# Softmax steps, M's combinations and w_out's block sums issued at other places in a fused recurrent-cross attention and SERF MLP kernel

## The chip, the cores and the metric

The kernel runs on one core of a Trainium2 chip. The metric is the device time of one execution in microseconds (us). One execution of the kernel before is laid open by the hardware profiler; all times inside the kernel that this document names come from that trace, counted from the start of its span.

Five engines matter: PE (TensorE, the matmuls; PEld is its weight load), DVE (VectorE), ACT (ScalarE), POOL (GpSimd) and SP (SyncE, which issues the DMAs). Each engine works through its own list of instructions in order; engines wait for each other through semaphores.

## The reference, cut to what matters

```python
def _attn_ref(x, state):                       # x (8, 8, 512, 64), state (8, 8, 32, 64)
    scale = 1.0 / np.sqrt(D)
    scores = scale * np.matmul(x, state.transpose(0, 1, 3, 2))
    a = softmax(scores)                        # (written out in the original)
    xread = np.matmul(a, state)
    scores2 = scale * np.matmul(state, x.transpose(0, 1, 3, 2))
    a2 = softmax(scores2)
    sread = np.matmul(a2, x)
    return np.concatenate([xread, sread], axis=2)

def _moe_ref(x, w_in, w_out):                  # x (4352, 512), w_in (512, 2048), w_out (2048, 512)
    h = x @ w_in
    sp = np.maximum(h, 0.0) + np.log1p(np.exp(-np.abs(h)))
    g = h * erf(sp)
    return g @ w_out
# the attention output, heads side by side, is the x of the second part; all in float32
```

## The kernel before

The eight batches are taken one after the other. For the 512 rows that come from `xread`, the kernel never forms the attention output: it multiplies M = state x w_in (made per batch, `mixed`) with the attention weights `aT`. Both large products, M x aT (the hidden layer h) and g x w_out, are done block-wise with seven products in place of eight (a fast 2 x 2 scheme), which needs sums of blocks: `combine_m` (of M), `combine_a` (of aT) and `combine_w` (of w_out, once for the whole kernel).

From batch 1 on a batch has four **groups**, g = 0 to 3. A group makes 512 hidden features for 256 tokens (`hidden7`, seven products of 128-column matmuls), applies softplus, Erf and the product with h (`finish`), and is multiplied into the output (`project7`, seven products of 256-column matmuls). The project step of a group is run one group later: its pieces are laid between the products of the next group's `hidden7`.

```python
    def hidden7(b, g, h, between):
        hs = act.tile([P, 4, S], F32, name="hs")
        s = act.tile([P, 4, S], F32, name="s")
        c11, c12, c21, c22 = (hs[:, k] for k in range(4))
        m1, u2, u3 = s[:, 3], c12, c21
        ...                                     # product(n, bank): matmuls, L457; softplus(k): L464
        add = lambda o, x, y: nc.vector.tensor_tensor(o, x, y, op=ALU.add)      # L465
        p, q = (ps_h.tile([P, S], F32, name="h") for _ in range(2))             # two PSUM banks
        product(1, p)
        nc.scalar.copy(m1, p)                   # L468
        product(6, q)
        add(u2, m1, q)
        between()
        product(2, p, False)                    # adds onto bank p: only after m1 was copied
        nc.scalar.copy(c11, p)                  # L473
        product(7, q, False)                    # adds onto bank q: only after u2
        add(u3, m1, q)
        softplus(0)
        between()
        p, q = (ps_h.tile([P, S], F32, name="h") for _ in range(2))             # the same two banks
        product(5, p)                           # only after c11 was copied
        add(c22, u3, p)
        product(4, q)                           # only after u3
        add(c21, u3, q)
        between()
        marks[:] = product(3, p, False), add(c12, u2, p)    # the group's last add; only after c22
        for k in (3, 2, 1):
            softplus(k)
        return s, hs

    def finish(s, hs):
        return (nc.scalar.activation(out=s, in_=s, func=ACTF.Erf),              # L507
                nc.vector.tensor_tensor(s, s, hs, op=ALU.mult))                 # L508

    def combine_w(g, last=False):               # block sums of w_out, L539; T[4], T[3] as the others
        ...
        if last:
            sub(T[3], B22, B12)
        else:
            sub(T[1], B12, B11)
            sub(T[2], B22, T[1])
            sub(T[4], B21, T[2])

    def project7(gT, hs, g, first, last, acc):  # L561 to L564 form S1..S4 on DVE, L565 the matmuls
        ...
        for n, (lhs, rhs, bank, c) in enumerate((
                (A12, B21, 0, 0), (A11, B11, 2, 0), (A22, T[4], 1, 0), (S2, T[2], 0, 1),
                (S3, T[3], 2, 1), (S1, T[1], 1, 1), (S4, B22, 3, 0))):
            ...
```

The softmaxes of batch b + 1 (`attention`) run inside the groups of batch b, in steps: scores (PE L197, copied by ACT L207), the maxima and first exponentials (DVE L217 to L221, ACT L222), the second exponentials (DVE L238 and L239, ACT L246), normalising and turning (DVE L228 to L233, L353), turning of the second weights (DVE L356 and DMAs) and the state read (PE L273, DVE L279). `combine_m` is DVE L397 to L400, `combine_a` L428 to L431, `mixed` PE L385 with copies on ACT L387 and DVE L388, and `store7` ACT L576 and DVE L575.

Where a step is issued is decided by the main loop. `side[n]` runs a step behind piece n of the pending project; pieces 0 to 2 lie inside `hidden7`, later ones behind it. `behind(marks, f)` makes the instructions of f be ordered behind the instructions in `marks`.

```python
    for b in range(1, B + 1):
        ...
        for g, (first, second) in enumerate(groups):
            side = {}
            if b < B and g == 0:
                side[2] = lambda turn=turn: next(turn)          # state read of this batch
            if b + 1 < B:
                if g == 0:
                    turn = attention(b + 1)
                    side[6 if b > 1 else 3] = lambda: behind(marks, next, turn)   # scores
                elif g == 1:
                    side[0] = lambda: [next(turn) for _ in range(4)]   # all other softmax steps
                else:
                    o = g - 2 ^ begins(b + 1)
                    side[4] = lambda: mixed(b + 1, 2 * o)
                    side[8] = lambda: (mixed(b + 1, 2 * o + 1), combine_m(b + 1, o))
                    if g == 3:
                        side[6] = lambda: combine_a(b + 1)
            ...                                                  # the last batches: not touched
            steps = accompanied(pending(), side)
            gT_ = first(lambda: next(steps))
            if b == 1 and g == 0:
                combine_m(1, 1 - begins(1))
                behind(marks, combine_w, begins(1))
            done(steps)
            if b == 1 and g == 0:
                combine_w(begins(1), True)
            if b == 1 and g == 1:
                behind(marks, combine_w, 1 - begins(1))
                behind(marks, combine_w, 1 - begins(1), True)
            ...
```

Up to batch 0's end (the first 122 us) the kernel loads and converts the weights and takes another, plain path; after batch 7 come the 256 rows of the states. Neither is touched.

Of the kernel before, what the change touches and what calls it, by code (L numbers as in the profile page):

```python
# [16 lines left out]
def kernel(  # L17
# [17 lines left out]
    nc = tc.nc  # L35
    B, H, S, D = x.shape
# [151 lines left out]
    marks = []  # L188
# [183 lines left out]
    def mixed(b, g, *copies):  # L372

        m_t[b, g] = mix.tile([P, 2, gw], F32, name="m")
        mixed_part(b, g, 0, 1, *copies)
# [14 lines left out]
    def combine_m(b, g):  # L390


        (X11, X12), (X21, X22) = ([m_t[b, 2 * g + j][:, e] for e in range(2)] for j in range(2))
        sx = mix.tile([P, 3, gw], F32, name="sx", bufs=2)
        S1, S2, S4 = (sx[:, k] for k in range(3))
        tt = nc.vector.tensor_tensor
        tt(S1, X21, X22, op=ALU.add)  # L397
        tt(S2, S1, X11, op=ALU.subtract)
        tt(X21, X11, X21, op=ALU.subtract)
        tt(S4, X12, S2, op=ALU.subtract)  # L400
        X[b, g] = X11, X12, S4, X22, S1, S2, X21
# [32 lines left out]

    X, Ys = {}, {}

    def hidden7(b, g, h, between):

# [6 lines that stand above are left out]
        def product(n, bank, first=True):  # L447
            x, y = X[b, g][n - 1], Ys[b][n - 1]
            for i in range(GF):
                q = slice(P * i, P * i + P)  # L450
                if b < B:
                    ops = [(x[:, q], y[:, h])]
                else:
                    ops = [(x[:, i // 2, k, P * (i % 2):P * (i % 2) + P], y[:, k])
                           for k in range(2)]
                for k, (lhsT, rhs) in enumerate(ops):
                    last = nc.tensor.matmul(out=bank[:, q], lhsT=lhsT, rhs=rhs,  # L457
                                            start=(first and i == 0 and k == 0),
                                            stop=(i == GF - 1 and k == len(ops) - 1),
                                            skip_group_check=not first)  # L460
            return last

        def softplus(k):
            nc.scalar.activation(out=s[:, k], in_=hs[:, k], func=ACTF.Softplus)  # L464
        add = lambda o, x, y: nc.vector.tensor_tensor(o, x, y, op=ALU.add)  # L465
        p, q = (ps_h.tile([P, S], F32, name="h") for _ in range(2))
        product(1, p)
        nc.scalar.copy(m1, p)  # L468
        product(6, q)
        add(u2, m1, q)  # L470
        between()
        product(2, p, False)
        nc.scalar.copy(c11, p)  # L473
        product(7, q, False)
        add(u3, m1, q)
        softplus(0)
        between()
        p, q = (ps_h.tile([P, S], F32, name="h") for _ in range(2))
        product(5, p)
        add(c22, u3, p)  # L480
        product(4, q)
        add(c21, u3, q)
        between()
        marks[:] = product(3, p, False), add(c12, u2, p)
# [3 lines that stand above are left out]
# [41 lines left out]
    B11, B12, B21, B22 = (wb[:, :, h, :, c, :] for h in range(2) for c in range(2))  # L529
    T = {}  # L530

    def combine_w(g, last=False):

        if not T:
            for k in 1, 2, 4:
                T[k] = act.tile([P, 2 * GF * P * 2], U32, name="raw", bufs=3).bitcast(F32) \
                    .rearrange("p (g i e) -> p g i e", i=GF, e=E2)
            T[3] = B12
        sub = lambda o, x, y: nc.vector.tensor_tensor(o[:, g], x[:, g], y[:, g], op=ALU.subtract)  # L539
        if last:  # L540
            sub(T[3], B22, B12)
        else:
            sub(T[1], B12, B11)
            sub(T[2], B22, T[1])
            sub(T[4], B21, T[2])

    def project7(gT, hs, g, first, last, acc):


        blocks = lambda t: [t[:, k].rearrange("p (i t) -> p i t", i=GF) for k in range(4)]  # L550
        A11, A21, A12, A22 = blocks(gT)
        S1, S2, S3, S4 = blocks(hs)
        tt = nc.vector.tensor_tensor
        for n, (lhs, rhs, bank, c) in enumerate((
                (A12, B21, 0, 0), (A11, B11, 2, 0), (A22, T[4], 1, 0), (S2, T[2], 0, 1),
                (S3, T[3], 2, 1), (S1, T[1], 1, 1), (S4, B22, 3, 0))):
            for i in range(GF):
                if i % 2 == 0 and n:
                    yield
                if i == 2 and n == 1:  # L560
                    tt(S1, A21, A22, op=ALU.add)  # L561
                    tt(S2, S1, A11, op=ALU.subtract)  # L562
                    tt(S3, A11, A21, op=ALU.subtract)
                    tt(S4, A12, S2, op=ALU.subtract)  # L564
                nc.tensor.matmul(out=acc[bank][:, E2 * c:E2 * c + E2], lhsT=lhs[:, i, :],  # L565
                                 rhs=rhs[:, g, i, :], start=(first and i == 0 and c == 0),
                                 stop=(last and i == GF - 1 and (c == 1 or bank == 3)))
# [37 lines left out]
    def begins(b):  # L605
        return 1 - b % 2

    def fast(b, parts, put):
        for h in range(parts):
            box = []  # L610

            def project_(gT, k, g, h, box):
                if k == 0:
                    box.extend(tiles(4))
                yield from project7(*gT, g, k == 0, k == 1, box)
                if k == 1:
                    store7(box, put(h))

            def first(g, h, between):
                gT = hidden7(b, g, h, between)  # L620
                finish(*gT)
                return gT
            for k in range(2):
                g = k ^ h ^ begins(b)
                yield lambda between, g=g, h=h: first(g, h, between), \
                    lambda gT, k=k, g=g, h=h, box=box: project_(gT, k, g, h, box)

    def done(steps):
# [9 lines left out]
    def behind(marks, f, *args):  # L638
        with ExitStack() as order:
            for m in marks:  # L640
                order.enter_context(tc.issue_after(m.ins))
            return f(*args)
# [97 lines left out]
    acc = tiles(NC)  # L740
# [85 lines left out]
    xT, _ = turn_x(1)  # L826
# [6 lines left out]
    turn = attention(1, xT)  # L833
# [51 lines left out]
    for b in range(1, B + 1):  # L885
        if b < B:
            groups = fast(b, 2, lambda h, b=b: put_x(b, h))
        else:
            groups = fast(b, 1, lambda h: put_s)
        for g, (first, second) in enumerate(groups):  # L890
            side = {}
            if b < B and g == 0:
                side[2] = lambda turn=turn: next(turn)
            if b + 1 < B:

                if g == 0:
                    turn = attention(b + 1)
                    side[6 if b > 1 else 3] = lambda: behind(marks, next, turn)
                elif g == 1:
                    side[0] = lambda: [next(turn) for _ in range(4)]  # L900
                else:
                    o = g - 2 ^ begins(b + 1)
                    side[4] = lambda: mixed(b + 1, 2 * o)
                    side[8] = lambda: (mixed(b + 1, 2 * o + 1), combine_m(b + 1, o))
                    if g == 3:
                        side[6] = lambda: combine_a(b + 1)
            elif b + 1 == B and g == 1:
                side[4] = lambda: [turn_read(range(k, min(k + 4, B))) for k in range(0, B, 4)]
            elif b + 1 == B and g > 1:

                if g == 2:
                    side[6] = lambda: combine_a(B)
                side[8] = lambda: combine_s(g - 2 ^ begins(B))
            steps = accompanied(pending(), side)
            gT_ = first(lambda: next(steps))
            if b == 1 and g == 0:
                combine_m(1, 1 - begins(1))
                behind(marks, combine_w, begins(1))
            done(steps)
            if b == 1 and g == 0:  # L920
                combine_w(begins(1), True)
            if b == 1 and g == 1:
                behind(marks, combine_w, 1 - begins(1))
                behind(marks, combine_w, 1 - begins(1), True)

            def pending(gT=gT_, second=second):
                return second(gT)
# [31 lines left out]
```

## Time and profile before

| what | value |
|---|---|
| time, median of 3 runs | 751.2 us (749.37 to 752.59) |
| span of the profiled execution | 749.4 us |
| granted TensorE clock, mean | 0.998 |
| PE busy | 730.8 us, 98% of the span |
| PE weight load busy | 584.4 us, 78% |
| DVE busy | 522.2 us, 70% |
| ACT busy | 388.6 us, 52% |

A busy share tells how long an engine had an instruction in it. Matmuls overlap in PE's pipeline, so a busy PE need not be a PE at its best rate; how fast it really goes is read from the timeline, as the distance from the start of one run of matmuls to the start of the next. Where PE stood and waited is told in the view of waits and in the timeline, in square brackets behind a run of matmuls, with the engine and line that released it.

In the trace a product of four matmuls of the program appears as eight, so a product of `hidden7` is "L457 ... x8", and one of `project7` "L565 ... x8".

### The profile page before, as it was taken

Reading aid. Unit: us, or ns where it says so; the run is one execution under the profiler, and the core shown is the slowest. Engines: PE = TensorE matmul, PEld = TensorE weight load, DVE = VectorE, ACT = ScalarE, POOL = GpSimd, SP = SyncE. Lnnn points to the kernel's source line nnn. Section 1 sums busy time; section 2 is a strip of 40 time slices with the busy share of each in tenths; the row PEclk is TensorE's granted clock in tenths of the full one; section 3 lists DMA queues with packets and bytes.
Section 4 is the critical chain, followed back from the end, with each engine's and each line's share of the span. In section 5 each row is a group of like instructions: output and inputs, shape, how many; then the busy total and the mean of one; then the engine's idle time right before and its main releaser. Section 6 shows DMA issues by size and latency. Waiting matters only on the chain.

```text
span 749.4 us, 12076 instructions
## 1 busy us (share of the span) xinstructions
PE 730.8 (98%) x4986; PEld 584.4 (78%) x4986; DVE 522.2 (70%) x763; ACT 388.6 (52%) x493; POOL 0.7 (0%) x6
## 2 busy tenths in 40 slices
PE   7899999889999999999999999999999999999997
PEld 6434435678888888888888888888888889999996
DVE  3987887897667665947687666766595765585523
ACT  3898794564356444463464445644456344443340
POOL 0000000000000000000000000000000000000000
PEclk9999999999999999999999999999999999999999
DMA  7577752521052002310061004300201000000001
GB/s 228 168 223 231 203 100 57 108 57 34 1 101 61 17 22 64 82 26 29 1 141 29 29 1 94 67 17 22 58 30 27 29 1 30 1 29 1 22 8 28
DMA packets 139166, 46.40 MB, mean 62 GB/s; under 512 B 126696, under 2 KB 130536, under 8 KB 139112
## 3 DMA queue, kind: packets, MB, share of 16 engines
q1 hardware_dynamic: 136744, 44.78, 23.9%
q10 hardware_dynamic: 2368, 0.85, 0.5%
q8 instruction: 39, 0.64, 0.4%
q14 instruction: 15, 0.12, 0.1%
HBM read 33.03 MB, written 8.91 MB: 56 GB/s over the span
## 4 chain that ended last, share of the span: by engine, by line
PE 78%; DVE 8%; ACT 1%; issue 0%; DVEq 0%
PE o L565 44%; PE h L457 24%; PE at L385 4%; PE o L513 3%; DVE hs L465 2%; PE at L197 1%; DVE aT L353 1%; PE h L674 1%; DVE xT L233 1%; DVE z L228 1%; DVE m L238 1%; PE at L273 1%; DVE xT L221 1%; ACT s L507 1%; DVE hs L562 0%; DVE hs L561 0%
## 5 line engine op out<-in xcount | busy, mean ns | idle before, releaser
L464 ACT ACTIVATE s<-hs 128x512 f32<-128x512 f32 x120 | 75.5, 630 | 99.0 <-DVE hs L465 98.6
L565 PE MATMUL o<-w_out,s 128*128 128x256 f32 x480 | 119.1, 382 | 0.0
L565 PE MATMUL o<-raw,hs 128*128 128x256 f32 x480 | 116.6, 384 | 0.0
L565 PE MATMUL o<-w_out,hs 128*128 128x256 f32 x480 | 114.5, 381 | 0.0
L508 DVE TENSOR_TENSOR s<-s,hs 128x2048 f32<-128x2048 f32 x30 | 68.7, 2291 | 65.6 <-ACT s L507 65.6
L565 PEld LDWEIGHTS o<-raw,hs 128*128 128x128 f32 x480 | 88.7, 190 | 30.1 <-issue 19.3
L565 PEld LDWEIGHTS o<-w_out,hs 128*128 128x128 f32 x480 | 90.4, 190 | 17.4 <-issue 4.2
L465 DVE TENSOR_TENSOR hs<-hs,h 128x512 f32<-128x512 f32 x90 | 61.2, 681 | 45.2 <-PE h L457 45.2
L565 PEld LDWEIGHTS o<-w_out,s 128*128 128x128 f32 x480 | 85.5, 193 | 8.2
L457 PEld LDWEIGHTS h<-aT,m 128*128 128x128 f32 x672 | 84.7, 192 | 9.3 <-ACT s L468 4.2
L457 PE MATMUL h<-aT,m 128*128 128x128 f32 x672 | 86.3, 276 | 3.1 <-ACT s L468 3.1
L465 DVE TENSOR_TENSOR hs<-s,h 128x512 f32<-128x512 f32 x60 | 40.9, 682 | 42.2 <-PE h L457 41.9
L468 ACT COPY s<-h 128x512 f32<-128x512 f32 x30 | 17.5, 585 | 97.1 <-PE h L457 97.1
L457 PE MATMUL h<-sy,sx 128*128 128x128 f32 x448 | 59.9, 277 | 1.4 <-ACT hs L473 1.4
L457 PEld LDWEIGHTS h<-sy,sx 128*128 128x128 f32 x448 | 57.0, 193 | 3.5 <-ACT hs L473 1.7
L513 PE MATMUL o<-w_out,s 128*128 128x512 f32 x128 | 58.9, 600 | 0.3 <-DVE s L687 0.2
L507 ACT ACTIVATE s<-s 128x2048 f32<-128x2048 f32 x30 | 57.3, 1911 | 0.3
L565 PE MATMUL o<-raw,s 128*128 128x256 f32 x240 | 56.8, 379 | 0.0
L473 ACT COPY hs<-h 128x512 f32<-128x512 f32 x30 | 17.6, 585 | 74.6 <-PE h L457 74.6
L565 PEld LDWEIGHTS o<-raw,s 128*128 128x128 f32 x240 | 43.9, 190 | 5.0
L513 PEld LDWEIGHTS o<-w_out,s 128*128 128x128 f32 x128 | 23.1, 190 | 30.7 <-issue 26.2
L464 ACT ACT_TABLE_LOAD x31 | 39.8, 1283 | 0.5
(118 smaller groups left out, 898.7 us busy)
## 6 DMA issues: line engine op xcount, KB each, us to landing
raw<-in_moe_w_in_dram SPq DMA_DIRECT2D x8, 1024.0 KB, 5.5
raw<-in_moe_w_out_dram SPq DMA_DIRECT2D x8, 1024.0 KB, 4.7
xq<-in_x_dram SPq DMA_DIRECT2D x112, 64.0 KB, 2.1
x<-in_x_dram SPq DMA_DIRECT2D x56, 128.0 KB, 2.8
out_dram<-ot SPq DMA_DIRECT2D x18, 256.0 KB, 2.0
sc<-xT SPq DMA_DIRECT2D x112, 32.0 KB, 1.9
out_dram<-ot SPq DMA_DIRECT2D x28, 128.0 KB, 1.7
x<-in_x_dram ACTq DMA_DIRECT2D x2, 256.0 KB, 5.7
```

The costliest lines, as they stand in the source:

```text
L197: on_pe = nc.tensor.matmul(out=s2[e][q, :], lhsT=st[r, b, q], rhs=xT[r, i, :], start=True, stop=True)
L221: nc.vector.tensor_tensor(a[:, e], a[:, e], over(m1[:, e]), op=ALU.subtract)
L385: nc.tensor.matmul(out=ps[e][q, :], lhsT=st[r, b, q], rhs=w_in[r, fs, i, :], start=True, stop=True)
L457: last = nc.tensor.matmul(out=bank[:, q], lhsT=lhsT, rhs=rhs, start=(first and i == 0 and k == 0), stop=(i == GF - 1 and k == len(ops) - 1 ...
L464: nc.scalar.activation(out=s[:, k], in_=hs[:, k], func=ACTF.Softplus)
L465: add = lambda o, x, y: nc.vector.tensor_tensor(o, x, y, op=ALU.add)
L468: nc.scalar.copy(m1, p)
L473: nc.scalar.copy(c11, p)
L507: return (nc.scalar.activation(out=s, in_=s, func=ACTF.Erf), nc.vector.tensor_tensor(s, s, hs, op=ALU.mult))
L508: nc.vector.tensor_tensor(s, s, hs, op=ALU.mult))
L513: nc.tensor.matmul(out=acc[r], lhsT=gT[:, i, P * r:P * r + P], rhs=w_out[:, GF * g + i, :], start=(g == 0 and i == 0), stop=(g == NG - 1 a ...
L565: nc.tensor.matmul(out=acc[bank][:, E2 * c:E2 * c + E2], lhsT=lhs[:, i, :], rhs=rhs[:, g, i, :], start=(first and i == 0 and c == 0), stop ...
```

## The change

It gives several DVE and ACT steps other places in the order; the arithmetic stays the same. There are four parts:

- In all batches from 2 on, the softmax steps behind the first exponentials are issued behind the last add of the group, and the first of them one step later in the group; before, all were issued at the start of group 1. They are meant not to stand between `hidden7`'s own adds and copies, for which PE waits.
- `combine_m` is issued one group later than the `mixed` that feeds it, behind the last add of that group; `combine_a` also goes behind a group's last add.
- In batch 1 everything of batch 2's attention comes one group later than in other batches, and group 1's two copies m1 and c11 go to DVE in place of ACT.
- In batch 1 the block sums of w_out (`combine_w`) are spread: T1 and T2 in group 0, T4 and T3 in group 1, the other half behind; and the seven products of the first project half of batch 1 run in the order 0, 1, 6, 3, 2, 5, 4, so that those that need the sums come late.

The diff, cut to its core:

```diff
-    def hidden7(b, g, h, between):
+    def hidden7(b, g, h, between, copy=nc.scalar.copy):
...
-        nc.scalar.copy(m1, p)
+        copy(m1, p)
...
-        nc.scalar.copy(c11, p)
+        copy(c11, p)
...
-    def combine_w(g, last=False):
+    def combine_w(g, *ns):
...
+        for n in ns:
+            sub(*{1: (T[1], B12, B11), 2: (T[2], B22, T[1]), 3: (T[3], B22, B12),
+                  4: (T[4], B21, T[2])}[n])
-    def project7(gT, hs, g, first, last, acc):
+    def project7(gT, hs, g, first, last, acc, order=range(7)):
...
+        for n, k in enumerate(order):
+            lhs, rhs, bank, c = products[k]
...
-                yield from project7(*gT, g, k == 0, k == 1, box)
+                yield from project7(*gT, g, k == 0, k == 1, box,
+                                    (0, 1, 6, 3, 2, 5, 4) if (b, h) == (1, 0) else range(7))
...
+            if 1 < b < B and g == 0:
+                side[3] = lambda: behind(marks, combine_m, b, 1 - begins(b))
             if b + 1 < B:
-                if g == 0:
+                late = b == 1
+                if g == late:
                     turn = attention(b + 1)
-                    side[6 if b > 1 else 3] = lambda: behind(marks, next, turn)
-                elif g == 1:
-                    side[0] = lambda: [next(turn) for _ in range(4)]
-                else:
+                    side[6] = lambda: behind(marks, next, turn)
+                if g == 1 + late:
+                    side[1] = lambda: next(turn)
+                    side[7] = lambda: behind(marks, lambda: [next(turn) for _ in range(3)])
+                if g > 1:
                     o = g - 2 ^ begins(b + 1)
                     side[4] = lambda: mixed(b + 1, 2 * o)
-                    side[8] = lambda: (mixed(b + 1, 2 * o + 1), combine_m(b + 1, o))
+                    side[8] = lambda: mixed(b + 1, 2 * o + 1)
                     if g == 3:
-                        side[6] = lambda: combine_a(b + 1)
+                        side[6] = lambda: behind(marks, combine_a, b + 1)
+                        side[3] = lambda: behind(marks, combine_m, b + 1, begins(b + 1))
...
-            gT_ = first(lambda: next(steps))
+            copy = [nc.vector.tensor_copy] if (b, g) == (1, 1) else []
+            gT_ = first(lambda: next(steps), *copy)
             if b == 1 and g == 0:
                 combine_m(1, 1 - begins(1))
-                behind(marks, combine_w, begins(1))
+                behind(marks, combine_w, begins(1), 1, 2)
+            if b == 1 and g == 1:
+                behind(marks, combine_w, begins(1), 4, 3)
             done(steps)
-            if b == 1 and g == 0:
-                combine_w(begins(1), True)
             if b == 1 and g == 1:
-                behind(marks, combine_w, 1 - begins(1))
-                behind(marks, combine_w, 1 - begins(1), True)
+                behind(marks, combine_w, 1 - begins(1), 1, 2, 4, 3)
```

More of the change, by code (lines that the diff above doesn't have):

```diff
@@ L539, in combine_w @@
         sub = lambda o, x, y: nc.vector.tensor_tensor(o[:, g], x[:, g], y[:, g], op=ALU.subtract)
-        if last:
-            sub(T[3], B22, B12)
-        else:
-            sub(T[1], B12, B11)
-            sub(T[2], B22, T[1])
-            sub(T[4], B21, T[2])
-    def project7(gT, hs, g, first, last, acc):
+        for n in ns:
+            sub(*{1: (T[1], B12, B11), 2: (T[2], B22, T[1]), 3: (T[3], B22, B12),
+                  4: (T[4], B21, T[2])}[n])
+    def project7(gT, hs, g, first, last, acc, order=range(7)):
         blocks = lambda t: [t[:, k].rearrange("p (i t) -> p i t", i=GF) for k in range(4)]
@@ L553, in project7 @@
         tt = nc.vector.tensor_tensor
-        for n, (lhs, rhs, bank, c) in enumerate((
-                (A12, B21, 0, 0), (A11, B11, 2, 0), (A22, T[4], 1, 0), (S2, T[2], 0, 1),
-                (S3, T[3], 2, 1), (S1, T[1], 1, 1), (S4, B22, 3, 0))):
+        products = ((A12, B21, 0, 0), (A11, B11, 2, 0), (A22, T[4], 1, 0), (S2, T[2], 0, 1),
+                    (S3, T[3], 2, 1), (S1, T[1], 1, 1), (S4, B22, 3, 0))
+        for n, k in enumerate(order):
+            lhs, rhs, bank, c = products[k]
             for i in range(GF):
@@ L614, in project_, with first @@
                     box.extend(tiles(4))
-                yield from project7(*gT, g, k == 0, k == 1, box)
+                yield from project7(*gT, g, k == 0, k == 1, box,
+                                    (0, 1, 6, 3, 2, 5, 4) if (b, h) == (1, 0) else range(7))
                 if k == 1:
                     store7(box, put(h))
-            def first(g, h, between):
-                gT = hidden7(b, g, h, between)
+            def first(g, h, between, *copy):
+                gT = hidden7(b, g, h, between, *copy)
                 finish(*gT)
@@ L624, in fast @@
                 g = k ^ h ^ begins(b)
-                yield lambda between, g=g, h=h: first(g, h, between), \
+                yield lambda *how, g=g, h=h: first(g, h, *how), \
                     lambda gT, k=k, g=g, h=h, box=box: project_(gT, k, g, h, box)
@@ L893 @@
                 side[2] = lambda turn=turn: next(turn)
+            if 1 < b < B and g == 0:
+                side[3] = lambda: behind(marks, combine_m, b, 1 - begins(b))
             if b + 1 < B:
-                if g == 0:
+                late = b == 1
+                if g == late:
                     turn = attention(b + 1)
-                    side[6 if b > 1 else 3] = lambda: behind(marks, next, turn)
-                elif g == 1:
-                    side[0] = lambda: [next(turn) for _ in range(4)]
-                else:
+                    side[6] = lambda: behind(marks, next, turn)
[3 more added lines that the diff above has]
+                if g > 1:
                     o = g - 2 ^ begins(b + 1)
                     side[4] = lambda: mixed(b + 1, 2 * o)
-                    side[8] = lambda: (mixed(b + 1, 2 * o + 1), combine_m(b + 1, o))
+                    side[8] = lambda: mixed(b + 1, 2 * o + 1)
                     if g == 3:
-                        side[6] = lambda: combine_a(b + 1)
+                        side[6] = lambda: behind(marks, combine_a, b + 1)
+                        side[3] = lambda: behind(marks, combine_m, b + 1, begins(b + 1))
             elif b + 1 == B and g == 1:
```

## The prediction

> **What bounds the kernel now.** I read the page first, then the waits of PE, a table by stages, and the timelines of PE, DVE and ACT around each wait.
>
> From the page, engine shares and the row of PE in 40 slices:
>
> ```profile
> PE 730.8 (98%) x4986; PEld 584.4 (78%) x4986; DVE 522.2 (70%) x763; ACT 388.6 (52%) x493; POOL 0.7 (0%) x6
> PE   7899999889999999999999999999999999999997
> ```
>
> PE is the bound; DVE and ACT matter only where PE waits for them. So the gain is at most the time in which PE stands or restarts. Its waits between 120 and 182 us, then between 182 and 625 us:
>
> ```profile
> PE h L457 <- ACT s L468: 3.1, 2, 1.9
> PE h L457 <- ACT hs L473: 1.4, 2, 0.7
> PE h L457 <- DVE hs L465: 0.4, 1, 0.4
> ...
> PE h L457 <- DVE hs L465: 0.9, 5, 0.2
> ```
>
> The columns are total us, times, longest. Batch 1 (groups at 121.95, 131.63, 157.94 and 180.88) has 4.9 us of waits; five later batches have one of 0.19 us each. By stages, two of batch 1's and a steady batch:
>
> ```profile
> 122.00:140.00 18.00, 15.38 (x162) 12.99 (x161) 14.21 (x18) 12.41 (x16) 0.00 (x0) 0.97 0.38 91
> 140.00:181.00 41.00, 38.80 (x243) 31.44 (x243) 34.58 (x52) 21.16 (x28) 0.00 (x0) 0.97 0.31 61
> 304.00:385.40 81.40, 81.22 (x595) 68.89 (x594) 58.11 (x90) 40.52 (x51) 0.00 (x0) 1.00 0.22 47
> ```
>
> The second number is PE's busy time. Busy time hides the restarts, so I take rates from distances between starts in the PE timeline. Two rows of an undisturbed stretch, then the waits of batch 1 and one of the small ones:
>
> ```profile
> 222.44 1.05 PE L457 MATMUL h<-aT,m 128*128 128x128 f32 x8
> 223.33 1.06 PE L457 MATMUL h<-sy,sx 128*128 128x128 f32 x8
> ...
> 136.56 1.16 PE L457 MATMUL h<-aT,m 128*128 128x128 f32 x8 [1.95 <-ACT s L468]
> 138.40 1.76 PE L457 MATMUL h<-sy,sx 128*128 128x128 f32 x8 [0.68 <-ACT hs L473]
> ...
> 150.61 1.16 PE L457 MATMUL h<-sy,m 128*128 128x128 f32 x8 [0.37 <-DVE hs L465]
> ...
> 162.06 1.16 PE L457 MATMUL h<-aT,m 128*128 128x128 f32 x8 [1.15 <-ACT s L468]
> 163.90 1.16 PE L457 MATMUL h<-sy,sx 128*128 128x128 f32 x8 [0.68 <-ACT hs L473]
> ...
> 233.76 1.16 PE L457 MATMUL h<-aT,sx 128*128 128x128 f32 x8 [0.19 <-DVE hs L465]
> ```
>
> A product of hidden7 goes at 0.89 us, one of project7 at 1.73 (8 matmuls), a visit to the small-tile matmuls (L197, L273, L385) at 1.02 plus about 0.1 on either side. Pure work between 121.95 and 180.88 (three groups): 21 products of hidden7 18.7, 14 of project7 24.2, batch 0's rest 3.4, four visits 4.1 and their switches 0.8: 51.2 us. It takes 58.9, so 7.7 us is all that batch 1 can give. A steady group without visits (222.44 to 241.36, 18.92) has 18.3 of work: 0.6 at most.
>
> Why PE waits at 136.56 is seen in the ACT timeline:
>
> ```profile
> 133.64 1.91 ACT L507 ACTIVATE s<-s 128x2048 f32<-128x2048 f32 x1
> 135.46 0.57 ACT L522 COPY ot<-o 128x512 f32<-128x512 f32 x1
> 135.92 0.59 ACT L468 COPY s<-h 128x512 f32<-128x512 f32 x1
> ```
>
> Product 1 is done at 132.5, but the copy of m1 stands behind ACT's Erf and a store copy until 136.5.
>
> [...] the page gives 276 ns for a matmul of L457 that comes every 111 ns. [...] the 128x512 copy takes 585 ns on ACT and 686 on DVE (L388), so moving it pays through its place, not its speed. [...] The trace has the 1283 ns; the copy at 223.53 is over at 224.11, the load starts at 224.13 and the exponential at 225.42, [...] I count 1.28.
>
> **The change part by part.** I took the order of instructions of the changed program on each engine, and walked through it with the distances that the trace shows: DVE 0.60 us for 512 elements, 0.33 for 256, 1.15 for 1024, 2.21 for 2048.
>
> *Batch 1, groups 0 and 1.* Group 0's last add ends at 131.58 as before. DVE then has T1 (to 132.75), m1's copy (133.4), T2, u2, c11's copy (135.8), and the 2048 product L508 (Erf is over at 135.55; 138.05). PE: product 2 at 133.5 and not 136.56, the state read 134.4, product 7 135.4, product 5 136.3, then a wait until L508 is there: the first L565 at 138.1 and not 139.95. From there PE runs through: product 4 at 140.7, product 3 at 142.5, and the rest of the projection. S4 is formed by 142.1 (needed 143.4); T4, now behind the group's last add (143.5 to 144.1), by 145.3 (needed 146.8); T3 by 146.4; the transpose L330 by 148.75, needed by the scores at 149.0. Group 2 starts at 153.2, not 157.94: 4.7 us won. All these are within 0.3 to 1.5 us of the need, on a DVE that has no pause.
>
> *Batch 1, group 2.* ACT now has only Erf and the two score copies before m1's copy, so the waits of 1.15 and 0.68 go (with their restarts 2.2 us). DVE, with the other half's sums and softmax steps between, gives u3 about 0.1 late and S4 about 0.7 late. Group 3 starts near 174.9 instead of 180.88: 6.0 won so far.
>
> *Batch 1, group 3.* Bank 2 is now finished last in the projection, so the store's copy L576 and add L575 come at the end, behind three S sums on DVE: bank 0 is free near 177.4, PE wants it at 176.7. 0.75 lost. Batch 1 gives 5.2 net.
>
> *Steady batches (2 to 6), group 1.* Before, c22's add stands on DVE behind the normalising steps (226 to 233.06). Now these are behind the last add; by my walk u3 ends 0.3 before product 4 wants it and c22 0.9 before product 3. The 0.19 goes, with its restart (233.41 to 233.76 and 0.1 after): 0.45. With a smoother order of group 2's first products, which the changed order shows, 0.5: five times, 2.4 us.
>
> *What it adds.* One ACT table load a batch (1.28) and two more in batch 1 group 2, where exponentials fall between softpluses; by my walk ACT's Erf there ends at 170.9 and its product is wanted at 176.7. ACT is 52% busy; nothing on the path. combine_m's four adds (2.4) move into groups 0 and 3, and put L508 of group 0 0.7 later, still 4 us ahead of its use.
>
> Sum: 5.2 + 2.4 = 7.6, 751.2 - 7.6 = 743.6. Hand walks ignore small latencies, mostly to the bad; I say 744.
>
> **The rivals.** (1) The wait is only replaced: DVE becomes batch 1's bound. For it: between 131.6 and 171 it has nearly no pause (38.8 of PE's 41 us stand beside 34.6 of DVE, which is to do the two copies as well). Then half of the gain is left: about 748. (2) A new wait in each steady batch: store adds, S sums and first exponentials still lie ahead of u3, with 0.3 us to spare, and the scores' transpose has 0.25 to spare. A miss by 0.5 in five batches: 746 to 747; a miss by 2, which I see no sign of, 754. (3) combine_a or M's sums come too late for the next batch. Against it: they are done some 10 us before their use, and the buffer of the sums is free once group 3's products are issued. (4) Softmax's transfer of the turned weights starts later; it has about 50 us before its use, so it is hidden.
>
> **Range and chances.** All of batch 1's loss and all steady restarts would give 7.7 + 5 x 0.6 = 10.7: 740.5 is the floor. 2% is 15 us, more than all that PE loses here, so "faster by over 2%" is nearly excluded. "Slower by over 2%" needs 2.5 us new in each of six batches. The walk's weakest links are rivals 1 and 2, so the range goes further up: 741 to 749.
>
> **What would show it.** Right: the two waits for ACT L468 and the two for L473 are gone; PE's idle time from 122 to 181 falls from 4.8 to under 2; the 0.19 waits for L465 are gone, and the distance from batch to batch falls from 81.41 to about 80.9; a first L565 near 138 and group 2 near 153. Wrong: waits of L457 for DVE L465 or of L565 for DVE L508, L539, L575 or L564 of more than 1 us in batch 1 (rival 1), or a distance between batches that stays or grows (rival 2).

## The result, and the profile after

The changed kernel takes 742.48 us (median of 4 runs, 742.32 to 742.61); the kernel before, run beside it, 750.33 us (4 runs, 749.37 to 752.59). The ratio is 0.9891, with a 95% interval from 0.9866 to 0.9916. Predicted were 744 us and a range of 741 to 749.

In the changed kernel the line numbers behind `combine_w` are smaller by two: its L563 is the L565 of before (matmuls of `project7`), L559 to L562 are the S sums (before L561 to L564), L573 and L574 the store (before L575, L576). First the shares of the engines on its page:

```profile
PE 727.6 (98%) x4986; PEld 583.9 (79%) x4986; DVE 523.5 (71%) x765; ACT 396.9 (54%) x498; POOL 0.7 (0%) x6
```

PE's share hardly moved, although the span fell by 9 us: the share is no measure of the gain. ACT has 8.3 us more to do (seven more table loads of 1.28, two copies fewer), and PE does not wait for it any more. These are all the waits of PE between 115 and 625 us:

```profile
PE o L563 <- DVE s L508: 0.4, 1, 0.4
PE o L563 <- DVE ot L573: 0.3, 1, 0.3
```

Before, there were 4.9 us in batch 1 and 0.9 later; now 0.7 us. The two that are left are the ones that the walk had named (the product L508 of group 0, and the late store). By stages, the part that stood worst, and a steady batch:

```profile
121.70:140.00 18.30, 17.94 (x179) 15.30 (x178) 14.56 (x22) 11.69 (x15) 0.00 (x0) 1.00 0.31 76
297.90:378.50 80.60, 80.60 (x593) 68.88 (x592) 58.11 (x90) 41.84 (x52) 0.00 (x0) 1.00 0.23 48
```

PE is busy for 17.94 of 18.30 us where it was for 15.38 of 18.00, and the granted clock (third number from the end) is 1.00 where it was 0.97. In PE's timeline, the place of the two long waits, and then the starts of groups 2 and 3 and the wait for the store:

```profile
133.24 1.16 PE L457 MATMUL h<-aT,m 128*128 128x128 f32 x8
134.32 1.10 PE L273 MATMUL at<-x,sc 128*32 128x64 f32 x64
135.36 1.16 PE L457 MATMUL h<-aT,m 128*128 128x128 f32 x8
136.35 1.06 PE L457 MATMUL h<-sy,sx 128*128 128x128 f32 x8
137.76 2.86 PE L563 MATMUL o<-w_out,s 128*128 128x256 f32 x12 [0.36 <-DVE s L508]
...
152.96 1.05 PE L457 MATMUL h<-aT,m 128*128 128x128 f32 x8
...
175.06 1.05 PE L457 MATMUL h<-aT,m 128*128 128x128 f32 x8
...
177.55 1.97 PE L563 MATMUL o<-w_out,s 128*128 128x256 f32 x8 [0.28 <-DVE ot L573]
```

Products 2, 7 and 5 now run while PE stood before. All starts, counted from batch 1's first product (121.95 before, 121.71 after), beside those of the walk:

| from batch 1's first product to | before | predicted | after |
|---|---|---|---|
| first matmul of the projection in group 1 | 18.00 | 16.15 | 16.05 |
| group 2 | 35.99 | 31.25 | 31.25 |
| group 3 | 58.93 | 52.95 | 53.35 |
| batch 2 | 79.70 | 74.5 | 74.68 |
| batch to batch, after that (81.41 before) | 81.41 | 80.9 | 80.67 |

So the 9.0 us between the two spans are 5.02 in batch 1, 3.69 in batches 2 to 6 (201.65 to 608.70 before, 196.39 to 599.75 after), 0.24 ahead of batch 1, where nothing was changed, and 0.05 behind. Of the 5.02, some 1.7 are neither waits nor restarts: the profiled execution of the kernel before ran for 3.4 us at a clock of 0.50, as is shown under e9.

### The profile page after: what moved, and what is told of

It is laid out like the page before. It is cut to its first block, busy times and chain, and to the rows that moved or that the text cites. A ratio compares the mean times of both kernels' runs of the same rounds, so it can differ in the third digit from the quotient of the medians.

```text
span 740.4 us, 12067 instructions
## 1 busy us (share of the span) xinstructions
PE 727.6 (98%) x4986; PEld 583.9 (79%) x4986; DVE 523.5 (71%) x765; ACT 396.9 (54%) x498; POOL 0.7 (0%) x6
## 4 chain that ended last, share of the span: by engine, by line
PE 85%; DVE 2%; ACT 1%; issue 0%
PE o L563 49%; PE h L457 26%; PE at L385 4%; PE o L513 3%; PE h L673 1%; PE at L197 1%; PE at L273 1%; DVE s L508 1%; ACT s L507 0%; DVE hs L465 0%; ACT L507 0%; DVE raw L539 0%; DVE xT L356 0%; DVE ot L573 0%; PE at L285 0%
## 5 line engine op out<-in xcount | busy, mean ns | idle before, releaser
L563 PE MATMUL o<-w_out,s 128*128 128x256 f32 x480 | 118.2, 380 | 0.6 <-DVE s L508 0.4
L563 PE MATMUL o<-raw,hs 128*128 128x256 f32 x480 | 116.2, 384 | 0.0
L563 PE MATMUL o<-w_out,hs 128*128 128x256 f32 x480 | 114.8, 380 | 0.0
L563 PEld LDWEIGHTS o<-raw,hs 128*128 128x128 f32 x480 | 89.1, 190 | 32.0 <-issue 21.0
L563 PEld LDWEIGHTS o<-w_out,hs 128*128 128x128 f32 x480 | 90.6, 190 | 17.1 <-issue 4.2
L465 DVE TENSOR_TENSOR hs<-hs,h 128x512 f32<-128x512 f32 x90 | 61.8, 687 | 59.3 <-PE h L457 59.0
L465 DVE TENSOR_TENSOR hs<-s,h 128x512 f32<-128x512 f32 x60 | 41.0, 684 | 73.3 <-PE h L457 73.3
L563 PEld LDWEIGHTS o<-w_out,s 128*128 128x128 f32 x480 | 84.6, 191 | 8.9 <-DVE s L508 0.5
L508 DVE TENSOR_TENSOR s<-s,hs 128x2048 f32<-128x2048 f32 x30 | 68.6, 2286 | 23.5 <-ACT s L507 23.5
L457 PE MATMUL h<-aT,m 128*128 128x128 f32 x672 | 84.6, 275 | 0.0
L468 ACT COPY s<-h 128x512 f32<-128x512 f32 x29 | 17.0, 585 | 100.5 <-PE h L457 100.5
L563 PE MATMUL o<-raw,s 128*128 128x256 f32 x240 | 56.8, 379 | 0.0
L473 ACT COPY hs<-h 128x512 f32<-128x512 f32 x29 | 16.9, 582 | 73.5 <-PE h L457 73.5
L563 PEld LDWEIGHTS o<-raw,s 128*128 128x128 f32 x240 | 43.5, 190 | 4.8
```

## The experiments

My theory: what is gained is the sum of separate PE delays, each of which has one cause in the order of DVE or ACT. Rivals: the parts need each other (batch 1's state is handed on); M's sums and not the softmax steps free the steady batches; on a DVE without a pause, a new place for one step only moves the delay to another. For the parts whose names don't tell it, the changed kernel is the base, and one thing in it is put back.

| run | what | median us | ratio to before, 95% interval | batch 1 | batch to batch |
|---|---|---|---|---|---|
| e1 | batch 1's own parts alone | 746.72 | 0.9943 (0.9923 to 0.9963) | 75.32 | 81.41 |
| e2 | batches 2 to 7 alone | 747.33 | 0.9955 (0.9941 to 0.9970) | 81.04 | 80.67 |
| e5 | sums of M and aT at old places | 743.68 | 0.9911 (0.9885 to 0.9936) | 75.32 | 80.78 |
| e3 | group 1's copies on ACT | 744.14 | 0.9918 (0.9888 to 0.9948) | 76.38 | 80.67 |
| e4 | plain order of products | 741.24 | 0.9870 (0.9853 to 0.9887) | 73.37 | 80.67 |
| e6 | new order in one projection only | 741.10 | 0.9871 (0.9853 to 0.9888) | 73.34 | 80.67 |
| e7 | w_out's sums at old places | 746.05 | 0.9937 (0.9917 to 0.9957) | 78.28 | 80.67 |
| e8 | batch 2's attention not late | 745.93 | 0.9946 (0.9917 to 0.9975) | 79.01 | 80.67 |
| e9 | kernel before, PE's pause filled | 749.50 | 0.9982 (0.9973 to 0.9991) | 77.98 | 81.42 |

"Batch 1" is the distance from its first product to batch 2's. The executions of e2, e7 and e8 differ by some us, and their granted clock with them: e2 takes 745.56 us at a clock of 1.000 and 748.70 at 0.994, e7 745.94 at 0.998 and 747.63 at 0.995, e8 744.94 at 1.000 and 750.05 at 0.993. The three have to be read with this in mind, and e9 deals with it. The runs were made at other times than the changed kernel's 742.48; the fastest executions of the kernel before were at 749.3 to 749.4 us each time, so that the medians can be compared. One more limit: the order of the instructions on an engine is not that of the source, as PE's in e4 shows below, so that putting one step back can move others too.

**e1 and e2: one half each.** In e1 the loop takes the old branches for all but batch 1's own parts; besides this edit it has that of e5 below:

```diff
-                    side[1] = lambda: next(turn)
-                    side[7] = lambda: behind(marks, lambda: [next(turn) for _ in range(3)])
+                    if b == 1:
+                        side[1] = lambda: next(turn)
+                        side[7] = lambda: behind(marks, lambda: [next(turn) for _ in range(3)])
+                    else:
+                        side[0] = lambda: [next(turn) for _ in range(4)]
```

In e2 those stay new, and batch 1's copies, order of products, block sums and attention are as before (the edits of e3, e4, e7 and e8 below, the second projection's block sums too, and the softmax steps in the old place `side[0]` for batch 1).

> Batch 1 as in the changed kernel; in batches 2 to 7 softmax steps, combine_m and combine_a at their old places. If the gains of the two parts add (my theory): the distance from batch 2's first product to batch 1's stays 74.7 us, from batch to batch it is 81.4 again with the 0.19 waits for L465 back; the time loses 5 x 0.73 = 3.6 us on the changed kernel, about 746. If batch 1's new order gave the steady batches their gain too (they inherit its state), the distance stays 80.7 and the time near 742.5.

> The complement: batch 1 as in the kernel before, batches 2 to 7 as in the changed one. My theory: waits of 3.1 for L468 and 1.4 for L473 are back, batch 1 takes 79.7 us again, the distance between later batches is 80.7; the time is 5.0 us above the changed kernel, about 747.5. If both parts are needed together, it is near 751.

Measured: e1 has the 81.41 again, with the five waits. From the waits of the weight loads of PE (PEld) in its batches 2 to 6:

```profile
PEld h L457 <- DVE hs L465: 2.9, 5, 0.6
...
PEld o L563 <- DVE hs L561: 1.3, 5, 0.3
```

These two rows are in the kernel before as well (there L565 and L563) and in neither e2 nor the changed kernel. The second is a wait that PE's own list doesn't show: S3 is formed late, the weight load stands 0.27 us, and the projection's step takes 1.83 in place of 1.73. e2 has the 80.67, and the waits for L468 and L473 of before. Its batch 1 takes 81.04 and not 79.7, and the clock was at 0.50 for longer (6.8 us, 3.4 in the kernel before). The halves add: 746.72 - 742.48 = 4.2 and 747.33 - 742.48 = 4.9, together 9.1, beside the 9.0 of the two profiles; by executions at a clock of 0.999 or 1.000 alone, 4.2 and 3.1 (745.6 for e2) are 7.3, beside 7.0 (749.5 for the kernel before). What one half does is not needed by the other. e1's batch 1 takes 75.32 where I had expected 74.7: M's sums had been put back in batch 1 too.

**e5: which of the steps frees the steady batches.**

```diff
-            if 1 < b < B and g == 0:
-                side[3] = lambda: behind(marks, combine_m, b, 1 - begins(b))
-                    side[8] = lambda: mixed(b + 1, 2 * o + 1)
+                    side[8] = lambda: (mixed(b + 1, 2 * o + 1), combine_m(b + 1, o))
-                        side[6] = lambda: behind(marks, combine_a, b + 1)
-                        side[3] = lambda: behind(marks, combine_m, b + 1, begins(b + 1))
+                        side[6] = lambda: combine_a(b + 1)
```

> The changed kernel with combine_m and combine_a alone at their old places. My theory: the softmax steps' place carries group 1's 0.58 us and the place of M's sums only the 0.11 of group 3 and at most 0.04 of group 2: distance between batches 80.8 to 80.85, group 1 still 18.34, group 3 back to 20.88, time 0.5 to 0.8 us above the changed kernel. Rival: M's sums carry the gain, then the distance returns to 81.2 or more and the time rises by 2.5 or more.

Measured: batch to batch 80.78, group 1 18.34 (219.70 to 238.04), group 3 20.87. So of the 0.74 us of a steady batch the softmax steps bring 0.63, the sums of M and aT together 0.10. The rival falls. In batch 1 the sums' old place costs another 0.64 us, in group 3, for which I had allowed nothing: 743.68, 1.2 above the changed kernel.

**e3: the two copies.**

```diff
-            copy = [nc.vector.tensor_copy] if (b, g) == (1, 1) else []
+            copy = []
```

> The changed kernel with group 1's two copies m1 and c11 of batch 1 on ACT again. Theory: m1's copy waits for ACT's Erf and a store copy (to about 136.4 us), so products 2, 7 and 5 can't fill PE's time ahead of L508; the first L565-kind matmul still comes near 137.8, but 1.8 us of products follow it instead of going before it; one wait for L468 of about 1.9 us is back, the L473 wait is not: time 1.5 to 2 us above the changed kernel. Rival: DVE is so full there that its two freed slots (1.2 us) pay for it: no difference.

Measured: 1.7 us above the changed kernel (744.14), batch 1 longer by 1.70. From its waits of PE:

```profile
PE h L457 <- ACT s L468: 1.9, 1, 1.9
...
PE o L563 <- DVE s L508: 0.2, 1, 0.2
```

The wait of the kernel before is back, the projection begins at the same time (15.98 us behind batch 1's first product, 16.05 in the changed kernel), and the 1.8 us of products 7 and 5 come behind it. On DVE the copy of m1 takes 0.69 us (at 132.49 in the changed kernel), on ACT 0.59 (at 135.92 in the kernel before), so 0.1 us longer; it gains by standing ahead of other work. The rival falls.

**e4 and e6: the order of the seven products.** In e4 the plain order stands everywhere, in e6 the new one for group 0's projection alone:

```diff
-                                    (0, 1, 6, 3, 2, 5, 4) if (b, h) == (1, 0) else range(7))
+  e4:                               range(7))
+  e6:                               (0, 1, 6, 3, 2, 5, 4) if (b, h, k) == (1, 0, 0) else range(7))
```

> The changed kernel with the seven products of every projection in the plain order 0 to 6. Theory: in group 1's pending projection (sums T3 and T4 not ready before 146.3 us) PE must wait about 1.5 us for T3 or T4 (L539); in group 2's, where the sums are long ready, the plain order ends bank 2 early and S4 late, which takes away the 0.28 wait for L573 and the late start of S4's product, 1.2 to 1.4 us. Together within 0.5 of the changed kernel. Rival: the order is needed in both groups, then over 1.5 us slower.

> The changed kernel with the new order of products only in the projection of group 0, and the plain order in that of group 1 (run inside group 2). Theory: no wait for L539, and the 0.28 wait for L573 with its restart (0.75) and the late S4 product (0.7 with two tile switches) go: 1.2 to 1.4 us below the changed kernel, 741.1 to 741.3. Rival: u3's and S4's lateness on a full DVE is merely moved to another product: no gain.

Measured: 741.24 and 741.10, both 1.2 to 1.4 us below the changed kernel. In e6 the wait for the store is gone and the only wait of PE between 115 and 630 us is the first of the two shown above. For group 0's projection I had expected e4 to wait 1.5 us for T3 or T4. It doesn't: its trace has the products in another order than its source, T4's (`raw,s`, from 146.93 us) behind one whose sum was ready (`raw,hs`, from 144.77). So the new order of products is worth nothing where it was meant to help, and costs 1.3 us in the second projection. Most of that is in group 2 (22.10 us in the changed kernel, 20.94 in e6), where the new order puts S4's product early and a visit to L385 is broken in two:

```profile
162.92 1.04 PE L385 MATMUL at<-w_in,st 64*32 64x512 f32 x2
163.89 1.99 PE L563 MATMUL o<-w_out,hs 128*128 128x256 f32 x8
165.82 1.08 PE L385 MATMUL at<-w_in,st 64*32 64x512 f32 x14
```

The two matmuls take 0.97 us, the fourteen 1.01; all sixteen at once take 1.02 in e6 (164.84 to 165.86). The late store costs less: group 3 goes from 21.33 to 21.15. That the earlier end of bank 2 is what frees the store is my reading; what e6 shows is that the wait of 0.28 us for L573 is gone. But now a weight load waits 0.30 us for u2 (L465), by the same reading behind these adds of the store, and group 3 is still 0.38 longer than in the kernel before (20.77).

e6 (or e4) beats both kernels: 1.3% below the one before.

**e7 and e8: is DVE near its limit in batch 1?** e7 puts combine_w back; e8 sets the scores of batch 2 into batch 1's group 0 again:

```diff
 e7
-                behind(marks, combine_w, begins(1), 1, 2)
-            if b == 1 and g == 1:
-                behind(marks, combine_w, begins(1), 4, 3)
+                behind(marks, combine_w, begins(1), 1, 2, 4)
+            if b == 1 and g == 0:
+                combine_w(begins(1), 3)
 e8
-                late = b == 1
+                late = False
-                    side[6] = lambda: behind(marks, next, turn)
+                    side[6 if b > 1 else 3] = lambda: behind(marks, next, turn)
```

> The changed kernel with combine_w at its old places (T1, T2, T4 behind group 0's last add, T3 right after, the other half behind group 1). On DVE m1's copy still comes early, but u2 and c11's copy now stand behind three sums and the 2048 product, to about 140.5 us and not 135.4. Theory: product 5 and product 4 come 3 us late and PE has only the first 12 matmuls of the projection to fill it: 1 to 2.5 us above the changed kernel, with waits for L465 or L473 in group 1. Rival: the sums' places are without effect because the projection fills the gap: within 0.3.

> The changed kernel, but batch 2's attention begins in batch 1's group 0, as in all other batches, and not one group later. Theory: on DVE the 2048 transpose L330 (2.2 us) then stands between T2 and the 2048 product L508 of group 0, while DVE has no pause there; the first L563-kind matmul comes near 139.2 and not 137.8, u2 and c11's copy near 140, so products 7 and 5 can't go ahead of it: 2 to 4 us above the changed kernel. Rival: the earlier scores relieve group 2 by as much, then within 0.5.

Measured: 746.05 and 745.93, 3.6 and 3.4 us above the changed kernel. e7's DVE timeline:

```profile
134.41 1.22 DVE L539 TENSOR_TENSOR w_out<-w_out 128x1024 f32<-128x1024 f32 x1
135.54 2.29 DVE L508 TENSOR_TENSOR s<-s,hs 128x2048 f32<-128x2048 f32 x1
...
138.13 1.22 DVE L539 TENSOR_TENSOR raw<-w_out,raw 128x1024 f32<-128x1024 f32 x1
139.26 0.68 DVE L465 TENSOR_TENSOR hs<-s,h 128x512 f32<-128x512 f32 x1
139.86 0.69 DVE L473 COPY hs<-h 128x512 f32<-128x512 f32 x1
```

u2 and c11's copy (L465, L473) come at 139.3 and 139.9, where the changed kernel has them at 134.2 and 134.8; PE waits 2.3 us for L508 and later 1.2 for the store. L508 itself is hardly later (135.54, after 135.43); the wait is longer because the products 7 and 5, which need u2 and c11's copy, no longer fill it. In e8 the transpose L330 stands in the same gap, and PE waits 1.2 us for it. So the rival of a full DVE is half right: DVE is full (in the changed kernel it has no pause from 131.3 to 142.3 us), and what e7 and e8 put ahead of u2 is paid for in PE's time; but the steps that the change moved were not needed there, which is why the delay did not move with them. Part of both times is clock. The executions at a clock of 1.00 stand at 745.0 for e8, 2.5 above the changed kernel; e7 had none, and by my estimate, with the 1.7 us of one fall of the clock (see e9) taken off, it would be 1.9 above. So e7's 3.6, over the 1 to 2.5 that I had expected, is not all a wait.

Within batch 1, then, the parts do not add as the two halves do, and my theory of separate delays fails there. e3, e7 and e8 each bring back a pause of PE in one and the same place, ahead of the first projection in group 1 (1.95, 2.28 and 1.16 us); their losses of 1.7, 3.6 and 3.4 us are together more than the 5.0 that batch 1 gained (with the clock's part taken off, by my estimate, 1.7 + 1.9 + 2.5 against 3.3). The copies on DVE, the spread sums and the later attention are each needed beside the others.

**e9: PE's pause and the clock.** In the kernel before, eight matmuls without use behind batch 1's state read:

```diff
+        fill = lambda t: [nc.tensor.matmul(out=t[:, 0:P], lhsT=ident, rhs=ident, start=True, stop=True) for _ in range(8)]
...
+        b == 1 and fill(ps_at.tile([P, S], F32, name="at"))
```

> The kernel before, with eight matmuls without use (identity times identity into a free PSUM tile) behind batch 1's state read, so that PE is not idle from 134.5 to 136.5 us; nothing else is meant to differ. Question: does the PE pause cause the lower granted clock that the trace of before shows from 138 to 144 us, and with it the spread of its times (749.3 to 752.6)? If so, the clock is 1.00 there and all runs lie within 0.5 us, near 749.5. If the clock falls for another cause, the spread stays 3 us.

The kernel before, by stages of 1 us in its profile:

```profile
138.00:139.00 1.00, 0.60 (x4) 0.60 (x5) 1.00 (x2) 0.98 (x2) 0.00 (x0) 0.89 1.01 227
139.00:140.00 1.00, 1.00 (x7) 1.00 (x7) 1.00 (x1) 0.99 (x2) 0.00 (x0) 0.50 0.49 106
140.00:141.00 1.00, 1.00 (x4) 0.82 (x4) 1.00 (x1) 0.29 (x1) 0.00 (x0) 0.50 0.97 220
141.00:142.00 1.00, 1.00 (x4) 0.82 (x3) 1.00 (x3) 0.00 (x0) 0.00 (x0) 0.50 0.06 13
142.00:143.00 1.00, 1.00 (x5) 0.81 (x4) 0.91 (x2) 0.00 (x0) 0.00 (x0) 0.91 0.58 100
```

and e9:

```profile
138.00:140.00 2.00, 1.07 (x5) 0.97 (x6) 2.00 (x2) 1.97 (x3) 0.00 (x0) 1.00 0.97 220
140.00:142.00 2.00, 2.00 (x23) 1.03 (x21) 2.00 (x3) 0.24 (x1) 0.00 (x0) 1.00 0.95 213
```

Before, the clock is at 0.50 from 139 to 142 us, right behind the waits of 1.95 and 0.68; summed over the five rows the missing clock is 0.11 + 3 x 0.50 + 0.09 = 1.7 us, which is half clock for 3.4 us. Ten matmuls of L565 take 3.36 us there (139.95 to 143.31), and 2.16 at their usual pitch. In e9 the clock stays at 1.00. Of its 12 runs ten stand at 749.36 to 749.69 with a clock of 0.999 or 1.000, two near 750.9 with 0.997; of 38 runs of the kernel before beside these experiments, 13 stand at 749.3 to 749.6, 16 at 750.7 to 751.3 (clock 0.998) and 9 at 752.4 to 752.6 (0.995). Of the 16 that ran beside e9, three stand at the first level. So the pause is what lowers the clock in most of them. My expectation was too strict for two of the twelve; kernels without the pause lose as much now and then, too (one execution in four of e4, e5 and e6, at 0.998). A limit: the eight matmuls also made the order of the next products a little different (the wait of 0.68 is gone, and PE waits 1.25 us for L508), so e9's time says nothing of its own; and not every fall of the clock is this one, since the profiles of e4 and e5 have theirs ahead of all that was changed (e4 0.57 and 0.58 in the two stages from 24 to 28 us, e5 a mean of 0.83 from 20 to 30). The changed kernel had a clock of 1.000 in all four runs.

## Why the prediction was right, point by point

**Batch 1, groups 0 and 1.** Predicted 4.7 us, measured 4.74, with each step of the walk within 0.3 us after the shift of 0.24 in the start (first L563 at 137.76, L330 at 146.18 to 148.5, group 2 at 152.96). The walk held because DVE has no pause from 131.3 to 142.3 us: its times there follow from the order and the distances alone. But the name was in part wrong. I called everything beyond the pure work waits and restarts; 1.7 us of it was a lower clock in the execution that was profiled. The 0.97 stood in the rows that I had quoted, and no step of the prediction used it. So the close match of the gain is in part luck: the walk gave the new times rightly, but beside an execution of the kernel before at full clock the gain here would have been about 3.0 us (4.74 - 1.7, an estimate).

**Batch 1, groups 2 and 3.** Predicted 6.0 won up to group 3 and 0.75 lost in it; measured 5.58 and 0.56. The waits for L468 and L473 in group 2 are gone as said. The two matmuls of L385 ahead of S4's product take 0.97 us, and L385's visit takes 1.98 us in its two pieces, where it takes 1.02 in one piece in e6; I had allowed 0.7 for a late S4. The loss in group 3 has the cause that was named, the late store, but with the store on time e6 has only 0.18 of it back; the larger loss, 1.16 us in group 2, is the one that could be avoided.

**Steady batches.** Predicted 0.5 a batch, 2.4 in all (five times 0.5 is 2.5); measured 0.74 and 3.69, which is more than the 0.6 a batch that I had called the most. The mechanism was right (e5: 0.63 of it by the softmax steps); the term was too small, because I looked only at the waits of PE. The weight loads' waits held two more delays of 0.1: S3 in group 1, and u2 behind M's sums in group 3 (two products take 1.89 us there before, from 265.69 to 267.58, and 1.78 after, from 259.80 to 261.58).

**What it adds.** Right: ACT's 8.3 us more cost nothing. The four adds of combine_m in groups 0 and 3 cost nothing either; group 0 takes 20.79 us in both kernels.

**The rivals.** None came in the changed kernel, but e7 and e8 show how near the first was: with one or two sums of 1.1 us or the transpose of 2.2 us put back, the product L508 goes ahead of u2 as well, u2 comes 5 us later, and over half of batch 1's gain is lost. The second had 0.3 us to spare by the walk; no wait for L465 is seen.

**The sum.** 7.6 predicted; 7.85 between the medians, 9.0 between the profiles. Both depend on how many executions of the kernel before were slowed by the clock: from its best runs (749.5) to the changed kernel's 742.5 it is 7.0 us.

## What to carry to other kernels

Where one engine sets the pace, walk the new order on the engines that feed it, with distances between starts taken from the trace: in these runs a step that DVE or ACT does "anyway" cost PE time where it stood ahead of the copy or add that PE needed next. A wait that is put down to one step can come from another that no longer fills the gap, as e7's for L508 does (2.28 us, 0.36 in the changed kernel). Look at the waits of the weight loads as well as of the matmuls, and at the clock column beside each wait. And when a change has several parts, try each alone: here one of them cost 1.3 us that the others hid, and putting back any one of three others took half of batch 1's gain or more.

## What the runs showed of the hardware that was not expected

In the profiles of before and e2 PE pauses for 1.95 us, works for 1.16 and pauses for another 0.68, and there the clock is at 0.50: for 3.4 us in before (138.8 to 142.2, reckoned from the stages of 1 us; it begins 0.4 us behind the second pause) and for 6.8 us in e2 (137.5 to 144.4; it begins as the second pause does). In the profiles of e4, e5, e7 and e8 the missing clock adds up to 1.7 us each, which at 0.50 is 3.4 us again (an estimate from their stages; e8 shows the 0.50 itself, from 140 to 142 us). By their times, 13, 16 and 9 of the 38 runs of the kernel before had no, one and about two such spells, so the same program meets the fall in some executions and not in others; with the first pause filled, ten of 12 had none (e9).

What sets the length of a spell, and how short a pause can be, no run shows. e7's single pause of 2.28 us stands ahead of the fall in its profile (0.54 from 138 to 140 us), and none of its four executions was at full clock (0.995 to 0.998); in e3 a pause of 1.95 us and one of 0.21 behind it go by at 1.00, and three of its four executions were at 0.999 or 1.000; in e9 one of 1.25 us goes by at 1.00.
